# 256 output columns of two row tiles computed behind the input gradient, and the first row tiles flipped in the middle of products

## The chip, the cores and the metric

One core of one Trainium2 chip runs the whole program. The metric is the device time of one execution in microseconds (us); lower is better. Kernels are compared only within the same rounds. A profiled execution has a span of its own, some 2 us shorter than the time measured from outside; spans are compared with spans and times with times.

In the profile PE is TensorE's matmul, PEld its weight load, DVE is VectorE, ACT ScalarE, POOL GpSimd, SP the queue from which most transfers are issued.

## The reference, cut to what matters

The program computes one layer and all its gradients. `S = 2048`, `D = 1024`, `F = 3584`; everything is bfloat16.

```python
xn  = layernorm(x)
y   = A(xn, k, v, ...)              # shift, long convolution, gating by xn
h   = relu(xn @ W_gate) * (xn @ W_up)
out = x + y_branch + h @ W_down      # output 0
# and, from grad_out: the gradients of x (output 1), k, v, the filters and the three weights
```

Three parts matter here. The first block of the hidden stage needs `xn` turned by 128x128 blocks ("flipped"), row tile by row tile, as the layer norm delivers it. `out` needs `h @ W_down`, and nothing else needs `out`. The gradient of `x` is the last stage, and ends for each row tile with the backward pass of the layer norm.

## The kernel before: the parts that matter

A row tile is 128 rows; there are 16. `pin` and `keep_in_program_order` hold an instruction behind the one traced before it on its engine; all others are placed by priority.

The layer norm is a generator in three steps per chunk; the first four chunks are one row tile each, the later ones two.

```python
def layer_norm(self, ...):
    for i, n in enumerate(self.LN_CHUNKS):          # (1, 1, 1, 1, 2, 2, ...)
        for j in range(n):
            total = row_sums(j, 0, ACT.Copy)         # ACT: sum of the row
            if i != 3 and i >= 2 and j == 0:
                self.tc.keep_in_program_order(total)
        ...                                          # mean
        for j in range(n):
            V.tensor_scalar(... op0=ALU.subtract)    # VectorE: x - mean
            row_sums(j, 2, ACT.Square)               # ACT: sum of squares
        yield
        ...                                          # variance, ACT.Sqrt
        yield
        ...                                          # 1/std, VectorE: scale the rows, store xn
        self.xn.append(xt[:, j, :])
        yield
```

A flip is eight transposes on TensorE into PSUM and a copy out of it on VectorE. The first block begins with 24 warm-up products on zeros, then:

```python
def flip(k):                     # flips row tiles until k are there
    while len(xT) < k:
        while len(self.xn) <= len(xT): next(ln)
        xT.append(self.flip_xn(len(xT)))

def first_gate_up(sp):           # two row tiles: gate, up, gate, up; 8 products of 512 columns each
    flip(sp + 1)
    gate(sp)
    flip(sp + 2)                 # before the up product
    while len(self.xn) < 4: next(ln)
    if sp == 2: chunk()          # all three steps of the norm of the fifth and sixth tiles
    up(sp)
    gate(sp + 1)
    up(sp + 1, (lambda: flip(3)) if sp == 0 else None)   # this one sits in the middle of the 8

for _ in range(5): next(ln)
flip(1)
next(ln); next(ln)
first_gate_up(0); first_gate_up(2)
chunk()                          # the norm of the seventh and eighth tiles
# then grad(sp): flip(min(sp + 6, HS)) ahead of the second product group
```

The last two stages: the output takes 2 x 28 products of 512 columns for each row tile, the input gradient 4 x 28; the last tile's second half is cut in two quarters.

```python
def out_phase(...):
    for st in range(16):
        hT = self.tall(h_d, st, "hT")        # transposed load of a row tile of h
        ...
        for ob in range(2):
            for kt in range(28):
                nc.tensor.matmul(ps[:], lhsT=hT[:, kt, :], rhs=self.wd[:, kt, oc], ...)
            nc.vector.tensor_tensor(out=o0[:, oc], in0=ps[:], in1=ya[:, oc], op=ALU.add)

def grad_x(...):
    for st in range(16):
        ggT = self.tall(...); guT = self.tall(...)   # same three buffers as hT
        cuts = (0, 512, 768, D) if last else (0, 512, D)
        ...                                          # products
        ...                                          # backward of the norm: VectorE, ACT, VectorE, store
```

Of the kernel before, what the change touches and what calls it, by code (L numbers as in the profile page):

```python
# [11 lines left out]
BF16 = mybir.dt.bfloat16  # L12
F32 = mybir.dt.float32
I32 = mybir.dt.int32
ALU = mybir.AluOpType
ACT = mybir.ActivationFunctionType
AX = mybir.AxisListType
P = 128
# [640 lines left out]
class LnMlp:  # L659
# [66 lines left out]
    def layer_norm(self, xn_d, jpool, jtag, spool):  # L726
# [4 lines left out]
        for i, n in enumerate(self.LN_CHUNKS):  # L731
# [27 lines left out]
            for j in range(n):  # L759
                total = row_sums(j, 0, ACT.Copy)  # L760
                if i != 3 and i >= 2 and j == 0:
                    self.tc.keep_in_program_order(total)
# [20 lines left out]
            for j in range(n):  # L783
                st = st0 + j
# [68 lines left out]
    def hidden(self, first, goT, load, ln, tables, Wg, Wu, Wd, g, xn_d, h_d, ug_d):  # L853
# [6 lines left out]
        for n in range(N):  # L860
# [61 lines left out]
            def first_gate_up(sp):  # L922

                flip(sp + 1)
                gate(sp)
                yield from step()
                flip(sp + 2)
                while len(self.xn) < 4:
                    next(ln)
                if sp == 2:  # L930
                    chunk()
                up(sp)
                yield from step()
                gate(sp + 1)
                yield from step()
                up(sp + 1, (lambda: flip(3)) if sp == 0 else None)
                yield from step()
# [24 lines left out]
            def grad(sp):  # L962
                for s in (sp, sp + 1):
                    if ahead and s == sp + 1:
                        flip(min(sp + 6, HS))
                    ps = self.ps_tile("ps_h")
                    self.gemm8(ps, gT[s], wd)
                    gh = self.e1_tile("gh")
                    self.pri.pin(nc.scalar.copy(out=gh[:], in_=ps[:]))  # L969
                    self.pri.pin(nc.vector.tensor_tensor(out=ru[s][:], in0=ru[s][:], in1=gh[:].rearrange(  # L970
                        "p (o f) -> p o f", o=1).to_broadcast([P, 2, 512]), op=ALU.mult))

                    def store(r=(s0 + s) * P, cols=cols, t=ru[s]):
                        self.pri.pin(nc.sync.dma_start(out=ug_d[r:r + P, :, cols], in_=t[:]))
                    self.defer(store)
                    yield 1730
                    self.tick()
# [9 lines left out]
            def chunk():  # L987
                with self.tc.issue_after(self.ln_act.ins):
                    for _ in range(3):
                        next(ln)  # L990

            if ahead:
# [4 lines left out]
                next(ln)  # L997
                flip(1)
                next(ln)
                next(ln)  # L1000
# [178 lines left out]

    def out_phase(self, x, xn_d, y_d, h_d, Wg, Wu, out0):  # L1180
        nc, tc, D = self.nc, self.tc, self.D
# [5 lines left out]
        for st in range(self.ST):  # L1187
# [15 lines left out]
            for ob in range(2):  # L1203
                oc = slice(ob * 512, ob * 512 + 512)
                ps = self.ps_tile("ps_o")
                for kt in range(self.FT):
                    nc.tensor.matmul(ps[:], lhsT=hT[:, kt, :], rhs=self.wd[:, kt, oc], start=(kt == 0),  # L1207
                                     stop=(kt == self.FT - 1))
                nc.vector.tensor_tensor(out=o0[:, oc], in0=ps[:], in1=ya[:, oc], op=ALU.add)
            nc.scalar.dma_start(out=out0[rows, :], in_=o0[:])  # L1210
# [3 lines left out]
    def grad_x(self, g, xn_d, y_d, ug_d, out1):  # L1214
# [3 lines left out]
        for st in range(self.ST):  # L1218
# [11 lines left out]
            V.tensor_tensor(out=gy[:], in0=gy[:], in1=gt[:], op=ALU.mult)  # L1230
            gx = p_ev.tile([P, D], F32, name="gx")
# [5 lines left out]
            last = st == self.ST - 1  # L1237
            cuts = (0, 512, 768, D) if last else (0, 512, D)
# [22 lines left out]
            for ob in range(2):  # L1261
# [3 lines left out]
                nc.sync.dma_start(out=out1[rows, oc], in_=o1[:, oc])  # L1265
        p_sm.release()
# [8 lines left out]
def kernel(  # L1275
# [79 lines left out]
    b.grad_x(g, xn_d, y_d, ug_d, out_1[0])  # L1355
# [30 lines left out]
```

## Time and profile before

| | before |
|---|---|
| median of the first 3 runs | 1927.05 us (1924.9 to 1928.51) |
| span of the profiled execution | 1922.2 us |
| granted TensorE clock, mean | 1.000 |
| last product ends, by the trace | 1915.56 us, 6.64 before the end |

The prediction below shows the page's head, the start and the end of the timeline. To those I add the page's list of what TensorE waits for (engine, what it was to do, line, releaser: us in total, times, the longest), cut:

```profile
PE pst_x L837 <- DVE ln_x L787: 2.0, 3, 1.4
PE ps_g L805 <- DMA wg<-in_B_W_gate_dram: 1.3, 3, 0.7
PE ps_g L805 <- DVE xnT L839: 0.4, 1, 0.4
```

The first line is the flips that wait for the norm's scaling (L787), the second the products of the third block that wait for a weight transfer at about 103 us, the third the first gate product that waits for the copy of its flipped tile. They are the waits at which the change aims, and one (the second) at which it doesn't.

One more line, from TensorE's timeline (start, duration, group), is the yardstick for the start of the kernel: the first gate products that use the fifth tile. All of the first block's flips that matter lie before it.

```profile
32.32 3.63 PE L805 MATMUL ps_g<-wg,xnT 128*128 128x512 bf16 x16
```

### The profile page before, as it was taken

Reading aid. Unit: us, or ns where it says so; the run is one execution under the profiler, and the core shown is the slowest. Engines: PE = TensorE matmul, PEld = TensorE weight load, DVE = VectorE, ACT = ScalarE, POOL = GpSimd, SP = SyncE. Lnnn points to the kernel's source line nnn. Section 1 sums busy time; section 2 is a strip of 40 time slices with the busy share of each in tenths; the row PEclk is TensorE's granted clock in tenths of the full one; section 3 lists DMA queues with packets and bytes.
Section 4 is the critical chain, followed back from the end, with each engine's and each line's share of the span. In section 5 each row is a group of like instructions: output and inputs, shape, how many; then the busy total and the mean of one; then the engine's idle time right before and its main releaser. Section 6 shows DMA issues by size and latency. Waiting matters only on the chain.

```text
span 1922.2 us, 36073 instructions
## 1 busy us (share of the span) xinstructions
PE 1888.9 (98%) x15350; PEld 886.8 (46%) x15582; DVE 909.1 (47%) x1366; ACT 635.0 (33%) x867; POOL 15.8 (1%) x38
## 2 busy tenths in 40 slices
PE   9999999999999999999999999999999999999998
PEld 4444444444444444444444444444444444444444
DVE  6777767767767754443444444310222222222222
ACT  5854354364364354354345344321000000000000
POOL 1100000000000000000000000000000000000000
PEclk9999999999999999999999999999999999999999
DMA  9975878974874972655662733386999854554551
GB/s 249 275 180 144 178 184 183 222 188 131 187 186 138 251 215 80 174 132 184 151 165 90 170 99 122 101 208 213 264 248 235 206 128 120 118 120 120 120 119 41
DMA packets 616018, 319.10 MB, mean 166 GB/s; under 512 B 450984, under 2 KB 585136, under 8 KB 615856
## 3 DMA queue, kind: packets, MB, share of 16 engines
q1 hardware_dynamic: 605360, 295.79, 63.6%
q10 hardware_dynamic: 9216, 16.78, 2.9%
q0 software_dynamic: 1280, 4.20, 0.6%
q8 instruction: 122, 2.00, 0.4%
q14 instruction: 40, 0.33, 0.1%
HBM read 141.56 MB, written 95.44 MB: 123 GB/s over the span
## 4 chain that ended last, share of the span: by engine, by line
PE 92%; issue 3%; ACT 2%; DVE 2%; DMA 1%; SPq 1%; ACTq 0%; DVEq 0%
PE ps_w L1053 19%; PE ps_x L1245 19%; PE ps_o L1207 10%; PE ps_h L805 9%; PE ps_u L805 9%; PE ps_g L805 9%; PE ps_d L1053 9%; PE ps L72 7%; PE ps_d L1066 1%; ACT ln_j L743 1%; PE pst L308 0%; PE ps_w L1066 0%; SPq L816 0%; DMA wu<-in_B_W_up_dram 0%; DMA ugs<-ug_d 0%
## 5 line engine op out<-in xcount | busy, mean ns | idle before, releaser
L1053 PE MATMUL ps_w<-ugs,xn_nat 128*128 128x512 bf16 x1672 | 375.9, 379 | 5.8 <-issue 4.3
L805 PEld LDWEIGHTS <-xnT 128*128 128x128 bf16 x1792 | 170.3, 98 | 210.6 <-issue 10.5
L1053 PEld LDWEIGHTS <-xn_nat 128*128 128x128 bf16 x1728 | 165.0, 98 | 199.4 <-issue 5.5
L1263 ACT ACTIVATE w<-xn,m 128x512 f32<-128x512 bf16 x32 | 24.3, 806 | 558.6 <-issue 316.8
L805 PE MATMUL ps_g<-wg,xnT 128*128 128x512 bf16 x869 | 203.8, 379 | 4.4 <-issue 1.6
L805 PE MATMUL ps_u<-wu,xnT 128*128 128x512 bf16 x866 | 203.7, 379 | 3.0 <-issue 1.3
L805 PE MATMUL ps_h<-wdT,goT 128*128 128x512 bf16 x863 | 202.4, 379 | 2.9 <-issue 1.8
L1245 PE MATMUL ps_x<-wgT,ggT 128*128 128x512 bf16 (+1 forms) x907 | 197.8, 372 | 0.9
L1245 PE MATMUL ps_x<-wuT,guT 128*128 128x512 bf16 (+1 forms) x906 | 197.6, 372 | 0.9
L1207 PE MATMUL ps_o<-wd,hT 128*128 128x512 bf16 x878 | 192.6, 379 | 0.9
L1053 PE MATMUL ps_d<-g_nat,hs 128*128 128x512 bf16 x741 | 167.4, 379 | 3.2 <-issue 2.7
L1245 PEld LDWEIGHTS <-ggT 128*128 128x128 bf16 x924 | 90.4, 98 | 103.3
L1245 PEld LDWEIGHTS <-guT 128*128 128x128 bf16 x924 | 90.4, 98 | 103.1
L1207 PEld LDWEIGHTS <-hT 128*128 128x128 bf16 x896 | 87.7, 98 | 105.7
L805 PEld LDWEIGHTS <-goT 128*128 128x128 bf16 x896 | 85.2, 98 | 102.6 <-issue 2.9
L319 DVE STREAM_TRANSPOSE flp<-C 128x1024 f32<-128x1024 f32 x48 | 90.5, 1931 | 83.4 <-ACT C L76 83.4
L908 DVE SCALAR_TENSOR_TENSOR ru<-ru,ps_u 128x512 bf16<-128x512 bf16 x112 | 76.5, 683 | 108.4 <-issue 43.0
L969 ACT CAST gh<-ps_h 128x512 bf16<-128x512 f32 x112 | 65.2, 583 | 164.1 <-PE ps_h L805 147.4
L1157 ACT CAST wi<-ps_w 128x512 bf16<-128x512 f32 x108 | 63.6, 589 | 161.8 <-PE ps_w L1053 153.1
L76 ACT CAST C<-ps 128x1024 bf16<-128x1024 f32 x96 | 92.5, 1015 | 69.0 <-PE ps L72 67.9
L319 DVE STREAM_TRANSPOSE flp<-B 128x1024 f32<-128x1024 f32 x48 | 90.9, 1939 | 48.6 <-ACT B L76 48.6
L1053 PEld LDWEIGHTS <-hs 128*128 128x128 bf16 x768 | 72.7, 98 | 88.9 <-issue 4.2
(170 smaller groups left out, 1469.4 us busy)
## 6 DMA issues: line engine op xcount, KB each, us to landing
ug_d<-ru SPq DMA_DIRECT2D x112, 256.0 KB, 4.0
ugs<-ug_d SPq DMA_DIRECT2D x112, 256.0 KB, 4.4
wg<-in_B_W_gate_dram SPq DMA_DIRECT2D x56, 256.0 KB, 4.4
wu<-in_B_W_up_dram SPq DMA_DIRECT2D x56, 256.0 KB, 4.8
h_d<-ht SPq DMA_DIRECT2D x112, 128.0 KB, 3.5
hs<-h_d SPq DMA_DIRECT2D x56, 256.0 KB, 5.1
out_dram<-wi SPq DMA_DIRECT2D x56, 256.0 KB, 2.5
gt<-in_grad_out_dram SPq DMA_DIRECT2D x32, 256.0 KB, 4.8
```

Source lines behind the costliest of these rows:

```text
L72: self.pri.pin(self.nc.tensor.matmul(out, lhsT=lhsT, rhs=rhs, start=start, stop=stop))
L76: self.pri.pin(self.nc.scalar.copy(out=out, in_=in_))
L319: self.pri.pin(self.nc.vector.transpose(out=df[:, c0:c0 + 32, :], in_=sf[:, c0:c0 + 32, :]))
L743: self.ln_act = nc.scalar.activation(out=jk[:, 0:cut], in_=xt[:, j, 0:cut], func=func, accum_out=sm[:, k, j:j + 1])
L805: self.pri.pin(self.nc.tensor.matmul(ps[:], lhsT=xT[:, kt * P:(kt + 1) * P], rhs=w(kt), start=(kt == 0), stop=(kt == self.DT - 1)), always ...
L908: self.pri.pin(nc.vector.scalar_tensor_tensor(out=ru[s][:, 1, :], in0=ru[s][:, 0, :], scalar=0.0, in1=ps[:], op0=ALU.is_gt, op1=ALU.mult))
L969: self.pri.pin(nc.scalar.copy(out=gh[:], in_=ps[:]))
L1053: self.pri.pin(self.nc.tensor.matmul(ps[:], lhsT=lhsT(st), rhs=rhs(st), start=(st == 0), stop=(st == self.ST - 1)))
L1157: self.pri.pin(nc.scalar.copy(out=wo[0][:, d, :], in_=ps[:]))
L1207: nc.tensor.matmul(ps[:], lhsT=hT[:, kt, :], rhs=self.wd[:, kt, oc], start=(kt == 0), stop=(kt == self.FT - 1))
L1245: nc.tensor.matmul(ps, lhsT=T[:, kt, :], rhs=W[:, kt, oc], start=(i == 0), stop=(i == n - 1))
L1263: nc.scalar.activation(out=w[:, oc], in_=xn[:, oc], func=ACT.Identity, scale=m[:, 7:8], bias=m[:, 6:7])
```

## The change

Two independent intents:

- **End.** The last 256 columns of the last two row tiles of the output are left out of the output stage and computed after the last input-gradient product, so that TensorE has work while the last backward pass of the norm runs on ACT and VectorE. Their weights, which the output stage's buffer no longer holds by then, are loaded again (1.8 MB) in the second input-gradient tile. The last tile is no longer cut in quarters.
- **Start.** The flips of the first tiles go from between two product groups into the middle of one (`gemm8` calls `mid` after four of eight products), so that each tile has 0.86 us more to arrive; the steps of the norm are traced in another order, and the second tile's row sum is pinned behind the first tile's square root.

The diff, cut to its core:

```diff
 # layer_norm
-                if i != 3 and i >= 2 and j == 0:
+                if i != 3 and i >= 1 and j == 0:
                     self.tc.keep_in_program_order(total)
 # first_gate_up
                 flip(sp + 1)
+                if sp == 2:
+                    chunk(1)
                 gate(sp)
                 yield from step()
-                flip(sp + 2)
-                while len(self.xn) < 4:
+                if sp == 0:
                     next(ln)
-                if sp == 2:
-                    chunk()
-                up(sp)
+                    next(ln)
+                    next(ln)
+
+                def mid():
+                    flip(sp + 2)
+                    while len(self.xn) < 4:
+                        next(ln)
+                    if sp == 2:
+                        chunk(2)
+                up(sp, mid)
 # grad
-                    if ahead and s == sp + 1:
-                        flip(min(sp + 6, HS))
                     ps = self.ps_tile("ps_h")
-                    self.gemm8(ps, gT[s], wd)
+                    self.gemm8(ps, gT[s], wd, (lambda: flip(min(sp + 6, HS))) if ahead and s == sp + 1 else None)
 # start of the first block
                 next(ln)
-                next(ln)
                 flip(1)
-                next(ln)
-                next(ln)
                 yield from first_gate_up(0)
 # out_phase
-            for ob in range(2):
-                oc = slice(ob * 512, ob * 512 + 512)
+            end = D if st < self.ST - 2 else D - self.REST          # REST = 256
+            for c0 in range(0, end, 512):
+                oc = slice(c0, min(c0 + 512, end))
 # new
+    def rest_load(self, x, xn_d, y_d, Wd):                          # called in tile 1 of grad_x
+        self.wdr = self.p_rest.tile([P, self.FT, self.REST], BF16, name="wdr")
+        for a in range(0, self.FT, 7):
+            nc.sync.dma_start(out=self.wdr[:, a:a + 7, :], in_=Wd[...])
+        t = self.p_rest.tile([P, 3, 2, self.REST], BF16, name="rest")
+        for i, src in enumerate((y_d, xn_d, x)):
+            nc.sync.dma_start(out=t[:, i], in_=src[(self.ST - 2) * P:self.S, c0:D]...)
+        ...                                                         # y * xn + x
+    def rest_out(self, h_d, out0):                                  # called after the last tile of grad_x
+        for i in range(2):
+            st = self.ST - 2 + i
+            hT = self.tall(h_d, st, "hT")
+            for kt in range(self.FT):
+                ins = nc.tensor.matmul(ps, lhsT=hT[:, kt, :], rhs=self.wdr[:, kt, :], ...)
+            nc.vector.tensor_tensor(out=t[:, 1, i], in0=ps, in1=t[:, 0, i], op=ALU.add)
+            nc.sync.dma_start(out=out0[st * P:(st + 1) * P, c0:D], in_=t[:, 1, i])
 # grad_x
-            cuts = (0, 512, 768, D) if last else (0, 512, D)
+            cuts = (0, 512, D)
```

More of the change, by code (lines that the diff above doesn't have):

```diff
@@ L985, in grad, with chunk @@
                         late.pop(0)()
-            def chunk():
+            def chunk(steps=3):
                 with self.tc.issue_after(self.ln_act.ins):
-                    for _ in range(3):
+                    for _ in range(steps):
                         next(ln)
@@ L1178, in tall @@
         return t
+    REST = 256
     def out_phase(self, x, xn_d, y_d, h_d, Wg, Wu, out0):
@@ L1202, in out_phase @@
             o0 = p_ev.tile([P, D], BF16, name="o0")
-            for ob in range(2):
-                oc = slice(ob * 512, ob * 512 + 512)
-                ps = self.ps_tile("ps_o")
+            end = D if st < self.ST - 2 else D - self.REST
+            for c0 in range(0, end, 512):
+                oc = slice(c0, min(c0 + 512, end))
+                ps = self.ps_tile("ps_o")[:, 0:oc.stop - c0]
                 for kt in range(self.FT):
-                    nc.tensor.matmul(ps[:], lhsT=hT[:, kt, :], rhs=self.wd[:, kt, oc], start=(kt == 0),
+                    nc.tensor.matmul(ps, lhsT=hT[:, kt, :], rhs=self.wd[:, kt, oc], start=(kt == 0),
@@ L1208, in out_phase @@
                                      stop=(kt == self.FT - 1))
-                nc.vector.tensor_tensor(out=o0[:, oc], in0=ps[:], in1=ya[:, oc], op=ALU.add)
-            nc.scalar.dma_start(out=out0[rows, :], in_=o0[:])
+                nc.vector.tensor_tensor(out=o0[:, oc], in0=ps, in1=ya[:, oc], op=ALU.add)
+            nc.scalar.dma_start(out=out0[rows, 0:end], in_=o0[:, 0:end])
         p_ev.release()
         self.p_wd.release()
-    def grad_x(self, g, xn_d, y_d, ug_d, out1):
+    def rest_load(self, x, xn_d, y_d, Wd):
+        nc, D, c0 = self.nc, self.D, self.D - self.REST
+        self.p_rest = self.tc.alloc_tile_pool(name="x_rest", bufs=1, side="right")
+        self.wdr = self.p_rest.tile([P, self.FT, self.REST], BF16, name="wdr")
+        for a in range(0, self.FT, 7):
+            nc.sync.dma_start(out=self.wdr[:, a:a + 7, :],
+                              in_=Wd[a * P:(a + 7) * P, c0:D].rearrange("(kt p) o -> p kt o", p=P))
+        t = self.p_rest.tile([P, 3, 2, self.REST], BF16, name="rest")
+        for i, src in enumerate((y_d, xn_d, x)):
+            nc.sync.dma_start(out=t[:, i], in_=src[(self.ST - 2) * P:self.S, c0:D].rearrange("(t p) o -> p t o", p=P))
+        nc.vector.tensor_tensor(out=t[:, 0], in0=t[:, 0], in1=t[:, 1], op=ALU.mult)
+        nc.vector.tensor_tensor(out=t[:, 0], in0=t[:, 0], in1=t[:, 2], op=ALU.add)
+        self.rest = t
@@ new lines, in rest_out @@
+    def rest_out(self, h_d, out0):
+        nc, D, c0, t = self.nc, self.D, self.D - self.REST, self.rest
+        for i in range(2):
+            self.pri.now()
+            st = self.ST - 2 + i
+            hT = self.tall(h_d, st, "hT")
+            ps = self.ps_tile("ps_r")[:, 0:self.REST]
+            for kt in range(self.FT):
+                ins = nc.tensor.matmul(ps, lhsT=hT[:, kt, :], rhs=self.wdr[:, kt, :], start=(kt == 0),
+                                       stop=(kt == self.FT - 1))
+                if kt == 0:
+                    self.tc.keep_in_program_order(ins)
+            nc.vector.tensor_tensor(out=t[:, 1, i], in0=ps, in1=t[:, 0, i], op=ALU.add)
+            nc.sync.dma_start(out=out0[st * P:(st + 1) * P, c0:D], in_=t[:, 1, i])
@@ L1215, in grad_x @@
+    def grad_x(self, x, g, xn_d, y_d, h_d, ug_d, Wd, out0, out1):
         nc, tc, D, V = self.nc, self.tc, self.D, self.nc.vector
@@ L1230, in grad_x @@
             V.tensor_tensor(out=gy[:], in0=gy[:], in1=gt[:], op=ALU.mult)
+            if st == 1:
+                self.rest_load(x, xn_d, y_d, Wd)
             gx = p_ev.tile([P, D], F32, name="gx")
@@ L1236, in grad_x @@
             hd = tc.keep_in_program_order
-            last = st == self.ST - 1
-            cuts = (0, 512, 768, D) if last else (0, 512, D)
+            cuts = (0, 512, D)
             for ob in range(len(cuts) - 1):
@@ L1265, in grad_x @@
                 nc.sync.dma_start(out=out1[rows, oc], in_=o1[:, oc])
+        self.rest_out(h_d, out0)
+        self.p_rest.release()
         p_sm.release()
@@ L1354 @@
     b.out_phase(x, xn_d, y_d, h_d, B_W_gate, B_W_up, out_0[0])
-    b.grad_x(g, xn_d, y_d, ug_d, out_1[0])
+    b.grad_x(x, g, xn_d, y_d, h_d, ug_d, B_W_down, out_0[0], out_1[0])
 _INS = ['A_q', 'A_k', 'A_v', 'A_shift_k', 'A_ssm_k', 'A_ssm_D', 'B_x', 'B_W_gate', 'B_W_up', 'B_W_down', 'grad_out']
```

## The prediction

The sum comes to -3.3 us for the end and -1.9 for the start, -5.2 together, from 1927.05 about 1922. The 216 and 109 ns per product and the 2.71 us of the last store in it are read from the trace of before.

> **What bounds the kernel now.** I read the page first, then the waits of TensorE, then its timeline over the first 60 us, then the timeline of all engines over the last 60 us, then the DMA issues. From the page:
>
> ```profile
> span 1922.2 us, 36073 instructions
> PE 1888.9 (98%) x15350; PEld 886.8 (46%) x15582; DVE 909.1 (47%) x1366; ACT 635.0 (33%) x867; POOL 15.8 (1%) x38
> PEclk9999999999999999999999999999999999999999
> ```
>
> TensorE is busy for 98% of the span at an ungated clock, so only two things can move the end: the number and width of its products, and the places where it stands still. The page says how little is there to win: 1922.2 - 1888.9 = 33 us of TensorE not busy in all, and part of those are records missing from the trace. The change touches two places, the start and the end. The start, in TensorE's own timeline (start, duration, group, and in brackets the idle time before it):
>
> ```profile
> 8.92 0.61 PE L837 MATMUL pst_x<-ident,ln_x 128*128 128x128 bf16 x8
> 9.96 1.90 PE L805 MATMUL ps_g<-wg,xnT 128*128 128x512 bf16 x8 [0.43 <-DVE xnT L839]
> 11.92 0.62 PE L837 MATMUL pst_x<-ident,ln_x 128*128 128x128 bf16 x8
> 15.83 1.03 PE L805 MATMUL ps_u<-wu,xnT 128*128 128x512 bf16 x4
> 17.01 0.62 PE L837 MATMUL pst_x<-ident,ln_x 128*128 128x128 bf16 x8 [0.15 <-DVE ln_x L787]
> 17.46 1.03 PE L805 MATMUL ps_u<-wu,xnT 128*128 128x512 bf16 x4
> 18.41 1.90 PE L805 MATMUL ps_g<-wg,xnT 128*128 128x512 bf16 x8
> 20.72 0.62 PE L837 MATMUL pst_x<-ident,ln_x 128*128 128x128 bf16 x8 [0.40 <-DVE ln_x L787]
> 26.36 1.89 PE L805 MATMUL ps_h<-wdT,goT 128*128 128x512 bf16 x8
> 29.65 1.07 PE L837 MATMUL pst_x<-ident,ln_x 128*128 128x128 bf16 x16 [1.41 <-DVE ln_x L787]
> 30.56 1.89 PE L805 MATMUL ps_h<-wdT,goT 128*128 128x512 bf16 x7
> ```
>
> The durations hold a modelled tail, so I count starts. Eight 512-wide products take 1.73 us from start to start (as from 14.10 to 15.83), eight transposes 0.45. By that count TensorE loses 0.59 us after the first tile's flip (8.92 + 0.45 to 9.96), 0.23 before the second tile's (9.96 + 1.73 to 11.92), 0.32 before the third's, 0.09 before the products at 18.41, 0.58 before the fourth's and 1.56 before the fifth's and sixth's. All of them wait for the layer norm, a chain over ACT and VectorE; between 9.96 and 30.56 that is 2.78 us. The end, from the timeline of all engines:
>
> ```profile
> 1902.96 3.15 PEld L1245 LDWEIGHTS <-ggT 128*128 128x128 bf16 x28
> 1912.34 3.22 PE L1245 MATMUL ps_x<-wuT,guT 128*128 128x256 bf16 x28
> 1915.60 0.42 DVE L1247 CUSTOM_DVE_ANT_0 gx<-ps_x,gy 128x256 f32<-128x256 f32 x1 [4.62 <-PE ps_x L1245]
> 1917.25 1.52 ACT L1263 ACTIVATE w<-xn,m 128x512 f32<-128x512 bf16 x2 [22.27 <-issue]
> 1918.09 1.40 DVE L1264 TENSOR_TENSOR o<-gx,w 128x512 bf16<-128x512 f32 x2 [0.55 <-ACT w L1263]
> ```
>
> The last product ends at 1915.56; then the layer norm's backward chain runs alone to 1918.09 + 1.40 = 1919.49, and a store to 1922.2: 6.64 us in which TensorE has nothing to do, 3.93 of chain and 2.71 of store.
>
> [...] 28 weight loads at full width span 6.04 us (216 each) and the half-width groups of the last tile 3.05 (109). Halving the width thus costs almost nothing in rate. [...] the first tile's copy out of PSUM starts at 9.49, only after two small layer-norm operations of the second tile (9.23 and 9.42) that stood ahead of it. [...]
>
> **The change, part by part.**
> Moved products. The last two row tiles of the output lose 256 of 1024 columns: per tile 28 products of 216 ns become 28 of 109, 6.04 to about 3.1 us, -5.8 us for two. They come back at the very end as 2 x 28 of 109 ns = 6.1 us, with some 0.1 for each change of group (the first half-width group took 3.15, later ones 3.05): 6.2. The last input-gradient tile is no longer cut in 512+256+256: its four half-width groups (3.15 + 3.05 x 3 = 12.3) become two full ones (12.1), -0.2. Sum on TensorE +0.2, close to nothing.
> The tail. The backward chain of the last tile (4.4 us at full width, by the tile before: 1891.29 to 1894.31 + 1.40) now lies beside 6.2 us of products. After the last product there remain one 256-wide addition from PSUM (0.42 us, as its neighbour of that width at 1915.60) and the store (2.7). So 3.93 becomes about 0.46: -3.5 us. Together with the +0.2: -3.3.
> The start. The first copy need no longer stand behind the second tile's variance: about -0.14 (copy at 9.35 in place of 9.49; the flip itself cannot come before 8.92, since the warm-up's last product starts at 8.71). Each flip then comes four products (0.86 us) later among the products, which covers the 0.23 wholly, and part of the 0.32 and 0.58: I take -0.23, -0.1, -0.4. The fifth and sixth tiles' sums are put ahead of a gate product, from 20.85 to about 18.8 on ACT, and their flips 0.86 later: 2.9 us of slack against a 1.56 us wait, of which I take -1.3, since ACT and VectorE, both some 70% busy there, may lose some of it. Against it: a flip in the middle leaves only 0.86 us until its tile is used, and the flip's own end plus a 0.69 us copy need 0.95 (17.46 to 18.41 now): +0.09 for two more tiles, and 0.1 where the copy finds VectorE busy. Sum -1.9.
> Sum of all: -3.3 - 1.9 = -5.2 us, from 1927.05 about 1922.
>
> **Rivals.** (1) A transposed load takes the place of the tail. The last rest product needs the last tile of h, whose buffer comes free when the last tile has used its gate gradient for the second time, 18.1 us into the tile; the product comes at 24.2 + 3.1 = 27.3. From the DMA issues:
>
> ```profile
> hT<-h_d SPq DMA_TRANSPOSE x16, 9.7
> guT<-ug_d SPq DMA_TRANSPOSE x16, 6.8
> ```
>
> 9.2 us are there against 6.8 for such a load in this stage (9.7 where other transposes ran beside it). I hold it for covered; if not, 0.5 to 2 us of the gain go: 1923 to 1924. [...]
> (2) The extra loads disturb the input gradient: 1.8 MB of weights plus 0.4 MB are queued during its second tile, ahead of that tile's transposed load. At some 200 GB/s, which the DMA row of the page shows elsewhere, 11 us, in a stage that moves only 115-120 GB/s; the load behind it has 12 us from issue to use. A stall of 1 to 2 us is possible, once. [...]
> (3) The start gains nothing: the norm chain is a chain, and if TensorE arrives earlier it waits for the next tile, or at the next weight block, whose weights already keep it waiting three times for 1.3 us in sum between 100 and 107 us while the DMA share is at its full. Then only the tail counts: 1924.
> (4) The start gains all 2.8 us, and the tail as said: 1921.
>
> **Range and chances.** The three times before lie between 1924.9 and 1928.5, so a median of few runs is uncertain by 1 to 2 us, as large as most of the terms. The centre is 1922.0; 8 in 10: 1918.5 to 1926. Two per cent are 38.5 us: more than all the time TensorE is not busy, so faster by over 2% can be all but ruled out; slower by over 2% would need the new order to upset the instruction stream of the middle 1800 us, which the change leaves alone and whose products are pinned in order.
>
> **What would show it.** Right: the last products are half-width and end 3 to 3.5 us before the span does, with a single addition and a store after them; the last tile's ACT pair lies beside products; TensorE busy stays within 1 us of 1888.9 but for missing records; the product group that now starts at 32.32 starts between 29.8 and 31. Wrong: idle time before the rest products with the transposed load of h as its releaser; an idle entry of some us in the second or third tile of the input gradient; longer waits for copies (xnT) before gate products in the first 30 us; or the waits for weights around 103 us grown by what the start gained.

## The result, and the profile after

Ratios are the mean time of one kernel's runs over the mean of the other's in the same rounds, so they are not quite the ratios of the medians quoted beside them.

| | before | after |
|---|---|---|
| first comparison, median | 1926.31 us (4 runs) | 1922.07 us (1919.92 to 1925.05, 4 runs) |
| ratio, 95% interval | | 0.9978 (0.9959 to 0.9997) |
| second comparison (run after_again), median | 1925.19 us (9 runs) | 1920.76 us (1919.8 to 1922.78, 5 runs) |
| ratio, 95% interval | | 0.9978 (0.9965 to 0.9992) |
| span of the profile | 1922.2 us | 1918.5 us |

So the change takes off 0.22%, some 4.2 us of 1926, in both comparisons. By the 2% measure that is "same"; the intervals show that it is real. The prediction was 1922.0, a gain of 5.2 us from 1927.05.

The head of the page of after:

```profile
span 1918.5 us, 36320 instructions
PE 1909.4 (100%) x15582; PEld 886.9 (46%) x15582; DVE 910.2 (47%) x1364; ACT 635.8 (33%) x867; POOL 15.7 (1%) x38
```

TensorE's busy time seems to have grown by 20 us. It hasn't: the trace of before holds 15350 of 15582 matmul records, this one all of them. The weight loads are complete in both, 886.8 and 886.9 us, and say that the work on TensorE is the same.

**The end**, from the timeline of all engines:

```profile
1908.62 6.21 PEld L1244 LDWEIGHTS <-hT 128*128 128x128 bf16 x56
1908.84 6.28 PE L1244 MATMUL ps_r<-wdr,hT 128*128 128x256 bf16 x56
1911.22 1.52 ACT L1301 ACTIVATE w<-xn,m 128x512 f32<-128x512 bf16 x2 [22.65 <-issue]
1913.01 0.68 DVE L1302 TENSOR_TENSOR o<-gx,w 128x512 bf16<-128x512 f32 x1
1915.15 0.42 DVE L1248 TENSOR_TENSOR rest<-ps_r,rest 128x256 bf16<-128x256 f32 x1 [1.46 <-PE ps_r L1244]
```

The 56 half-width products end at 1908.84 + 6.28 = 1915.12; the ACT pair and the last VectorE addition of the norm's backward pass lie beside them and are done at 1913.69. What is left is one 256-wide addition and a store. From the last product to the end it is now 1918.5 - 1915.12 = 3.38 us, before it was 6.64. There is no bracket on the product line: they waited for nothing.

**The start**, from TensorE's timeline (in brackets the idle time before the group and what ended it):

```profile
9.63 0.61 PE L837 MATMUL pst_x<-ident,ln_x 128*128 128x128 bf16 x8
...
17.59 0.62 PE L837 MATMUL pst_x<-ident,ln_x 128*128 128x128 bf16 x8 [0.30 <-DVE ln_x L787]
...
21.60 0.61 PE L837 MATMUL pst_x<-ident,ln_x 128*128 128x128 bf16 x8
22.05 1.03 PE L805 MATMUL ps_u<-wu,xnT 128*128 128x512 bf16 x4
23.79 1.90 PE L805 MATMUL ps_g<-wg,xnT 128*128 128x512 bf16 x8 [0.71 <-DVE xnT L839]
...
29.84 1.06 PE L837 MATMUL pst_x<-ident,ln_x 128*128 128x128 bf16 x16
...
31.62 3.63 PE L805 MATMUL ps_g<-wg,xnT 128*128 128x512 bf16 x16
```

The waits for the norm are gone before the second flip, before the fourth (21.60) and before the fifth and sixth (29.84, 1.56 us by starts before). The third still waits, and a new wait stands before the fourth tile's gate product: its four up products start at 22.05 and take 0.86 us, so it could start at 22.91 and starts at 23.79. The list of waits says the same in sums, and shows the wait for the weights grown from 1.3 to 1.6 us:

```profile
PE ps_g L805 <- DMA wg<-in_B_W_gate_dram: 1.6, 1, 1.6
PE ps_g L805 <- DVE xnT L839: 1.0, 2, 0.7
PE pst_x L837 <- DVE ln_x L787: 0.3, 1, 0.3
```

Waits for the norm and the copies went from 2.4 to 1.3 us, and the fifth tile's gate product starts at 31.62 in place of 32.32.

**Where the span's 3.7 us went.** Last product 1915.56 to 1915.12: 0.44 us from the start, less the grown weight wait and some 0.2 us of extra products. Behind the last product: 3.26 us. The gain is nearly all the end's.

### The profile page after: what moved, and what is told of

It reads as the page before. It is cut to its first block, busy times and chain, and to the rows that moved or that the text cites. A ratio compares the mean times of both kernels' runs of the same rounds, so it can differ in the third digit from the quotient of the medians.

```text
span 1918.5 us, 36320 instructions
## 1 busy us (share of the span) xinstructions
PE 1909.4 (100%) x15582; PEld 886.9 (46%) x15582; DVE 910.2 (47%) x1364; ACT 635.8 (33%) x867; POOL 15.7 (1%) x38
## 4 chain that ended last, share of the span: by engine, by line
PE 96%; DVE 1%; ACT 1%; DMA 1%; issue 0%; POOL 0%; SPq 0%; ACTq 0%; POOLq 0%
PE ps_x L1283 20%; PE ps_w L1056 20%; PE ps_o L1214 10%; PE ps_h L805 9%; PE ps_u L805 9%; PE ps_g L805 9%; PE ps_d L1056 9%; PE ps L72 7%; PE ps_d L1069 1%; PE ps_w L1069 1%; ACT ln_j L743 1%; PE ps_warm L851 0%; PE pst L308 0%; PE ps_r L1244 0%; DMA wg<-in_B_W_gate_dram 0%
## 5 line engine op out<-in xcount | busy, mean ns | idle before, releaser
L1056 PE MATMUL ps_w<-ugs,xn_nat 128*128 128x512 bf16 x1728 | 383.9, 379 | 0.0
L1283 PE MATMUL ps_x<-wgT,ggT 128*128 128x512 bf16 x896 | 198.6, 379 | 0.0
L1283 PE MATMUL ps_x<-wuT,guT 128*128 128x512 bf16 x896 | 198.6, 379 | 0.0
L1214 PE MATMUL ps_o<-wd,hT 128*128 128x512 bf16 (+1 forms) x896 | 187.6, 372 | 0.0
L1056 PE MATMUL ps_d<-g_nat,hs 128*128 128x512 bf16 x768 | 172.1, 379 | 0.0
```

The source lines that it names most:

```text
L1056: self.pri.pin(self.nc.tensor.matmul(ps[:], lhsT=lhsT(st), rhs=rhs(st), start=(st == 0), stop=(st == self.ST - 1)))
L1214: nc.tensor.matmul(ps, lhsT=hT[:, kt, :], rhs=self.wd[:, kt, oc], start=(kt == 0), stop=(kt == self.FT - 1))
L1283: nc.tensor.matmul(ps, lhsT=T[:, kt, :], rhs=W[:, kt, oc], start=(i == 0), stop=(i == n - 1))
```

## The experiments

The theory after the result: the end gives what was predicted; the start gives less than half, because a copy now stands behind other VectorE work and one flip still waits. Rivals: the start did gain, but the weight wait at 103 us takes it back; or the start is bound by something not yet seen. Twelve runs. Each variant shares its rounds with the kernel before.

### 1. The change again, and its parts alone

`after_again` is the changed kernel. `tail_only` keeps the new end and has the old start; `start_only` the reverse (the edits are the two halves of the diff above, undone). `one_rest` leaves 256 columns of one tile instead of two for the end:

```diff
-            end = D if st < self.ST - 2 else D - self.REST
+            end = D if st < self.ST - 1 else D - self.REST
-        t = self.p_rest.tile([P, 3, 2, self.REST], BF16, name="rest")
+        t = self.p_rest.tile([P, 3, 1, self.REST], BF16, name="rest")
         ...                                                         # rows of one tile loaded, not of two
-        for i in range(2):
-            st = self.ST - 2 + i
+        for i in range(1):
+            st = self.ST - 1 + i
```

> The changed kernel once more, to tell its gain from the spread of single executions (four runs lay between 1919.9 and 1925.1 us). Theory (tail -3.3 us, start -0.7 to -1.4, nothing given back): 4 to 4.7 us below the kernel before. Rival (the start's gain is given back at the weights waited for near 103 us, only the tail counts): about 3.3. Profile: 3.4 us from the end of the last product to the end of the span; from the first flip to the first gate product of the fifth tile 22.0 us (23.4 before), whatever the moment at which the warm-up ends.

> The start as before, the output's last columns moved behind the input gradient. Theory: -3.3 us against the kernel before, all of it in the tail (6.6 us from last product to end become 3.4), first flip to the fifth tile's gate product 23.4 us as before. Rival (the tail was not what was gained, the moved products cost as much as they hide): within 1 us of before.

> The flips in the middle of products and the new order of the norm, the end as before. Theory: -0.7 to -1.4 us against the kernel before; first flip to the fifth tile's gate product 22.0 us; 6.6 us from last product to end. Rival (later waits for weights take it back): 0, with the waits for wg near 103 us grown by about 1 us over the 1.3 us of before.

> Only the last row tile leaves 256 columns, so 28 half-width products (3.1 us) follow the last input-gradient tile in place of 56 (6.2 us). Theory: the last tile's backward chain (4.4 us) is then longer than the products beside it; the additions of the input gradient are the last work again, the end comes about 4.4 + 0.4 + 2.7 us after the last input-gradient product, and the time is 0.7 to 1.1 us above the changed kernel. Rival (any products behind the last tile do, since the store sets the end): the same time as the changed kernel.

| run | median us (range, 5 runs) | ratio to before (95%) | span |
|---|---|---|---|
| after_again | 1920.76 (1919.8 to 1922.78) | 0.9978 (0.9965 to 0.9992) | 1919.0 |
| tail_only | 1921.41 (1920.34 to 1922.8) | 0.9981 (0.9969 to 0.9994) | 1919.5 |
| start_only | 1924.42 (1923.96 to 1926.38) | 0.9997 (0.9985 to 1.001) | 1924.6 |
| one_rest | 1921.49 (1919.48 to 1925.13) | 0.9982 (0.9969 to 0.9994) | 1917.7 |

The end alone is worth 0.19%, 3.7 us of 1925.19; the start alone 0.03%, 0.6 us, which its interval doesn't tell from nothing. The two add up to the whole within the noise. One expectation failed: from the first flip to the fifth tile's gate product I foresaw 22.0 us whatever the moment at which the warm-up ends; it took 22.54 in `after_again` and 22.65 in `start_only` (the account of the prediction below says why).

`one_rest` shows why two tiles and not one. From its timeline:

```profile
1909.88 3.15 PEld L1244 LDWEIGHTS <-hT 128*128 128x128 bf16 x28
1914.26 0.68 DVE L1302 TENSOR_TENSOR o<-gx,w 128x512 bf16<-128x512 f32 x1
```

The 28 products are over by about 1913.3, but the backward pass ends at 1914.94: it is longer than what lies beside it, and sets the end again. To put sizes on one scale I take, for each variant, the time from the first of the moved products to the end, less what the output stage saved. What was saved is read from the length of the output stage, 193.4 us before. For after: 9.88 - 5.9 = 4.0. For `one_rest`: 7.82 - 2.9 = 4.9, so 0.9 worse. (Its profile has the shortest span of all for other reasons: its wait for the weights at 103 us was only 1.19 us. Its time over five runs is not better.)

### 2. The copy behind other work, and the weights at 103 us

In after, VectorE does this around the fourth tile's copy:

```profile
22.25 0.88 DVE L766 TENSOR_SCALAR ln_x<-ln_x,ln_s 128x1024 bf16<-128x1024 bf16 x2 [0.33 <-DVE ln_s L764]
23.05 0.68 DVE L839 COPY xnT<-pst_x 128x1024 bf16<-128x1024 bf16 x1
```

The transposes start at 21.60. Before, the copy followed the same transposes after 0.66 us (20.72 and 21.38), which would be 22.26 here. But the subtraction for the fifth and sixth tiles (two instructions) stands ahead of it, because the change traces `chunk(1)` before that flip and the copy is kept in program order. On ACT, the third tile's square root is late in the same way, behind the fourth tile's row sum:

```profile
14.53 1.04 ACT L743 ACTIVATE ln_j<-ln_x 128x1024 bf16<-128x1024 bf16 x1
15.57 0.19 ACT L774 ACTIVATE ln_s<-ln_b 128x1 f32<-128x1 bf16 x1
```

`split4_pin3` mends both: the row sum is pinned behind the root, and the subtraction is traced after the copy.

```diff
-                if i != 3 and i >= 1 and j == 0:
+                if i >= 1 and j == 0:
                     self.tc.keep_in_program_order(total)
             ...
+            if i == 4:
+                yield
             for j in range(n):
-                V.tensor_scalar(out=xt[:, j, :], ..., op0=ALU.subtract)
+                centred = V.tensor_scalar(out=xt[:, j, :], ..., op0=ALU.subtract)
+                if i == 4 and j == 0:
+                    self.tc.keep_in_program_order(centred)
             ...
-                        chunk(2)
+                        chunk(3)
```

`wgfirst_after` and `wgfirst_before` test the rival on the changed and the old kernel. On the SP queue, the transfer of the third block's gate weights stands behind a load of `xn` for the other branch, which is issued late. The edit moves that load and the load after it behind the weights, without touching the order of the arithmetic:

```diff
-        yield 13000
+        yield 21990
         self.load_xn(nx)
         ...
-        yield 9000
+        yield 10
```

`all3` is `split4_pin3` and this edit together.

> The changed kernel with the two waits of its start taken away by order alone: the subtraction of the fifth and sixth tiles' means stands behind the fourth tile's copy out of PSUM on VectorE (it stood ahead of it, and the gate product after it waited 0.71 to 0.72 us), and the fourth tile's row sum stands behind the third tile's square root on ACT (it stood ahead of it, and the third flip waited 0.30 to 0.77 us). Theory: first flip to the fifth tile's gate product 21.99 - 0.8 - 0.4 = 20.8 us, the time 1 us below the changed kernel's. Rival (the norm is one chain, so what is taken from one tile's wait comes back at the next): 21.7 us or more, the time unchanged.

> The changed kernel; on the queue of transfers the load of normalised rows that waits for their store (4.4 us near 90) and what follows it stand behind the weights of the third block in place of ahead of them; the compute engines' order is the same. Theory: TensorE's wait for these weights near 103 us (1.2 to 2.4 us in six profiles, in one of them followed by a stretch at a lower clock) goes, and with it part of the spread: 1 to 2.5 us below the changed kernel, 5.5 to 7 below the kernel before. Rival (the wait comes from the transfer engines' load at that time, not from the place in the queue): wait and time as in the changed kernel.

> The same move in the kernel before, to see whether the change's gain depends on this wait. Theory (the wait moves along with TensorE and takes nothing back of the change's gain): 1 to 2.5 us below the kernel before, and the kernel of the same move with the change stays 4 to 4.8 us below this one. Rival (the wait takes back the gain of the start): the difference between the two with the move is 1 us larger than without it, 5 to 6 us.

> Both mends of the changed kernel together (the two orders of the start, the weights of the third block first). Theory: they add up: 7 us below the kernel before, near 1918. Rival: no better than the better of the two alone.

| run | median us (range, 5 runs) | ratio to before (95%) | span |
|---|---|---|---|
| split4_pin3 | 1922.68 (1920.83 to 1924.27) | 0.9978 (0.9965 to 0.9992) | 1922.4 |
| wgfirst_after | 1921.73 (1921.19 to 1923.75) | 0.9978 (0.9966 to 0.9991) | 1922.0 |
| wgfirst_before | 1924.44 (1924.26 to 1926.67) | 0.9993 (0.998 to 1.0005) | 1922.6 |
| all3 | 1921.55 (1921.03 to 1922.51) | 0.9976 (0.9963 to 0.9988) | 1919.2 |

Before in these rounds: 1926.3, 9 runs.

`split4_pin3` did half of what it was to do. In it the fourth tile's gate product starts at 22.75, 1.04 us earlier than in after (and earlier than in any of the seven profiles with the change's start, 23.31 to 23.79), but it still waits 0.63 us: only the first of the two subtractions was pinned behind the copy, and the scheduler put the other one ahead. The fifth tile's gate product starts at 31.05 with a wait of 0.33 for its copy. From the first flip to the fifth tile's gate product it is 22.99 us, where I had expected 20.8, and the time didn't move: the rival held. My theory of the copies explains the waits, not the time: the mended wait came back in part as a later one.

For the weights, `wgfirst_after` did remove the wait for `wg`. TensorE's list of waits between 86 and 115 us now begins with another:

```profile
PE ps_u L805 <- DMA wu<-in_B_W_up_dram: 2.0, 2, 1.8
```

The gate weights were issued at 94.65 in place of 98.89, but the `up` weights only at 102.50, behind the loads that had been moved. In this profile, then, the wait passed from one weight to the next. Between 100 and 110 us, without the move, the sixteen transfer engines are at their full share, 1.08 to 1.12 by the profile's windows, and move 294 to 329 GB/s (start_only, after and tail_only); that this load sets the wait is not shown. For in `wgfirst_before` the wait for `wu` is only 0.7 us, and in `all3` the list from 90 to 130 us has no weights at all (one group of its up products does take 2.48 us from start to start in place of 1.73), and still the time moved by nothing that is clear of the noise. In these two TensorE waits for VectorE's transposes of the other branch instead (`flp`, 2.0 and 1.8 us from 115 us on), a wait that before and after don't have: what was gained was waited for again later. The forecasts for `all3` (1918) and `wgfirst_after` (1 to 2.5 us below the changed kernel) failed; their rivals held. The two kernels with the move differ by 2.7 us (medians), which neither my 4 to 4.8 nor the rival's 5 to 6 had: taking this wait away uncovers no hidden gain of the start.

Does this wait give back what the start gained? The load of `xn` that stands first was issued 0.61 us after the other branch's transposes began on TensorE, before (94.78 and 95.39) and after (94.25 and 94.86), and 0.61 to 1.23 in the other profiles with the queue's old order; the gate weights followed it at 99.52 before and 98.89 after, 0.63 earlier. So their issue moves along with TensorE, by as much as the start gained. The rival doesn't hold as a systematic effect, though the wait itself varies between profiles from 1.0 to 2.4 us: when the transfer lands, the traces don't explain.

### 3. All copies first; flips alone; other widths

`copies_first` goes further with the copies: both subtractions of chunks 4 and 5 are pinned behind the copies, and the norm of the seventh and eighth tiles is traced later.

```diff
-            if i == 4:
+            if i in (4, 5):
                 yield
             ...
-                if i == 4 and j == 0:
+                if i in (4, 5):
                     self.tc.keep_in_program_order(centred)
             ...
                 yield from first_gate_up(2)
-                chunk()
+                chunk(1)
             ...
                 yield from grad(sp)
+                if ahead and sp == 0:
+                    chunk(3)
```

(against `split4_pin3`). `flip_mid` moves only the flips into the middle of products, with the steps of the norm that are traced beside them, and leaves the norm's order and pins as in the kernel before; it has the new end. `rest128` and `rest512` leave 128 and 512 columns for the end (`REST = 128`, `REST = 512`).

> The changed kernel; on VectorE both subtractions of the fifth and sixth tiles' means stand behind the fourth tile's copy out of PSUM, both of the seventh and eighth behind the fifth's and sixth's copies, and the fourth tile's row sum on ACT behind the third tile's square root (in the first try at this only one of two subtractions was moved, and a gate product still waited 0.61 to 0.63 us for its copy). Theory: the waits for copies (0.71 to 0.72 us before the fourth tile's gate product, 0 to 0.87 before the fifth's) go, the fifth tile's gate product starts near 30.5 to 30.8 us in place of 31.2 to 32.3, the time is about 1 us below the changed kernel's. Rival (the norm is one chain; what is put off for the copies makes later flips wait): the product at 31.2 or later, or the seventh tile's flip waits; time as the changed kernel.

> Only one part of the start: the flips go into the middle of products, the order of the norm stays as before; the end is the changed kernel's. Compare with the kernel that has the old start and the new end (fifth tile's gate product at 32.54 us, waits for normalised rows of 2.7 us). Theory: a flip that comes 0.86 us later waits that much less, but the chain before it is as late as before: the waits for rows fall to about 1 us and the copies now cost 0.1 to 0.7 each; the fifth tile's gate product near 31.9, 0.5 to 0.7 us of the start's gain. Rival A (the middle flips are the whole gain): near 31.6 or below, as in the changed kernel. Rival B (the norm's new order is the whole gain): 32.4.

> Only 128 columns of the last two tiles at the end, so 56 products 128 wide follow. Theory: at 57 ns each, as the flips run, they take 3.2 us, less than the 4.4 us of the backward chain beside them, which becomes the end again: 0.8 to 1.3 us above the changed kernel. Rival (the weight load of 98 ns sets the pace of so narrow products): they take 5.5 us and end after the chain, but the tiles of the output gain only 3 us for it: 2.4 us above the changed kernel.

> 512 columns of the last two tiles at the end: 56 full-width products, 12.1 us, behind the last input-gradient tile, and 3.7 MB of weights and 0.8 MB of rows loaded during its second tile in place of 2.2 MB. Theory: the tail is one addition of 512 columns (0.69 in place of 0.42 us) and a store of twice the size, 0.3 to 0.5 us more; if the loads run at the 200 GB/s or so of the changed kernel (2.2 MB from 1530.5 to 1542.3) they take 22 us and the second tile's transposed load, queued behind them, is late: a wait of 2 to 6 us appears before a product of the second or third tile, in sum 2 to 6 us above the changed kernel. Rival (the loads do not get in the way of the transposed one): 0.3 to 0.5 us above.

| run | median us (range, 5 runs) | ratio to before (95%) | span |
|---|---|---|---|
| copies_first | 1921.14 (1920.17 to 1922.26) | 0.9975 (0.9962 to 0.9988) | 1920.5 |
| flip_mid | 1923.3 (1921.12 to 1925.82) | 0.9984 (0.997 to 0.9997) | 1921.8 |
| rest128 | 1922.62 (1920.7 to 1926.73) | 0.9985 (0.9972 to 0.9997) | 1921.6 |
| rest512 | 1921.83 (1921.53 to 1922.77) | 0.9979 (0.9966 to 0.9991) | 1919.7 |

Before in these rounds: 1926.31, 9 runs.

**`copies_first`** removes every listed wait between the first copy and the fifth and sixth flips, and then stops. TensorE, and ACT's row sum for the seventh tile:

```profile
22.34 1.90 PE L809 MATMUL ps_g<-wg,xnT 128*128 128x512 bf16 x8
28.39 1.06 PE L841 MATMUL pst_x<-ident,ln_x 128*128 128x128 bf16 x16
32.37 3.63 PE L809 MATMUL ps_g<-wg,xnT 128*128 128x512 bf16 x16 [2.05 <-DVE xnT L843]
```

```profile
28.32 1.06 ACT L743 ACTIVATE ln_j<-ln_x 128x1024 bf16<-128x1024 bf16 x1 [2.72 <-DMA ln_x<-in_A_q_dram]
```

TensorE is 1.45 us earlier than in after, both at the fourth tile's gate product (22.34 for 23.79) and at the fifth and sixth flips (28.39 for 29.84), and the fifth tile's gate product is none the earlier: 32.37, where the kernel before had 32.32. ACT had run out of rows: it could go on with those of the seventh and eighth tiles only at 28.3 us. On VectorE, the step of their norm that follows stood ahead of the copies for the fifth and sixth tiles again. Here the start runs into a load. It is visible in other profiles too. Wherever else ACT had to wait for those rows, the fifth tile's gate product came a fixed time after ACT went on:

| run | ACT goes on | fifth tile's gate product | between |
|---|---|---|---|
| after | 26.85 | 31.62 | 4.77 |
| start_only | 26.78 | 31.55 | 4.77 |
| wgfirst_after | 27.57 | 32.34 | 4.77 |
| rest512 | 27.88 | 32.65 | 4.77 |
| all3 | 26.71 | 31.49 | 4.78 |

In after, the chain between is short enough to read: ACT's two row sums, VectorE's mean (29.07) and subtraction (29.48, 0.88 us), then a product of the gradient (30.28), then the two copies (30.88). In the kernel before, ACT was busy until 27.5 us with other work, so a landing at 27 could not be seen. The load isn't the limit everywhere: in after TensorE's own work would have let the product start at 30.74 + 0.86 = 31.60, so it lost nothing, and in after_again, one_rest and rest128 ACT did not wait for the rows at all. TensorE's wait for the copies behind it was 0.23 us in start_only, 0.83 in all3, 0.87 in wgfirst_after, 1.37 in rest512 and 2.05 here. Part of the lateness lies on the SP queue: the load stands there behind transposed loads, whose issuing instructions ended at 20.3 us in after and at 23.1 here; it was issued at 20.46 and 23.23, and ACT went on 6.39 and 5.09 us later (6.08 in start_only, issued at 20.70). No run shows what an earlier issue would bring.

**`flip_mid`** shows that moving flips is not enough. The fifth and sixth flips still wait 1.13 us for the norm and the gate product behind them 0.99 us; it starts at 32.91, later than in the kernel before, and later than my 31.9 and both rivals had it. The gain of the start needs the norm's new order as well.

**The widths.** On the scale of experiment 1 (time from the first moved product to the end, less what was saved): `rest128` 8.1 - 2.9 = 5.2, `one_rest` 4.9, after 4.0, `rest512` 16.2 - 12.0 = 4.2. With 3.1 and 3.3 us of products beside it the backward pass, 4.4 us long, sticks out; with 6.2 it is covered, and more products bring nothing. From the timeline of `rest128`:

```profile
1913.51 3.33 PEld L1244 LDWEIGHTS <-hT 128*128 128x128 bf16 x56
1918.27 0.28 DVE L1248 TENSOR_TENSOR rest<-ps_r,rest 128x128 bf16<-128x128 f32 x1
```

Its 56 products cost 3.3 us, under 60 ns each, although each weight load by itself is recorded with 98 ns: loads overlap, and I had held it possible that they don't. The end is late because the last addition (1918.27) stands behind the backward pass on VectorE, not for the products. The width of the last store hardly matters: from the end of the last addition to the end of the span it is 3.05 us with 32 KB (`rest128`), 2.93 with 64 (after) and 3.02 with 128 (`rest512`). In `rest512` the larger reload might have held up the input gradient's transposed load, and 2 to 6 us were expected for that. In the trace the instruction that issues this load takes 9.68 us, in after 3.59, but TensorE waits only 0.23 us for it:

```profile
1547.05 5.82 PEld L1283 LDWEIGHTS <-guT 128*128 128x128 bf16 x28 [0.23 <-DMA guT<-ug_d]
```

So doubling the moved work, and the bytes, costs some 0.2 us on this scale: the choice of 256 columns of two tiles is at the edge of a flat stretch. The times order the same way (0.9978 and 0.9979 against 0.9982 and 0.9985), but no two of these intervals are apart.

None of the twelve beats the changed kernel clearly; `copies_first` (0.9975) and `all3` (0.9976) lie within its interval.

## Why the prediction was right, and the step that was mis-sized

**Right.** The bound: TensorE, busy for 98% and 100% of the span at a mean granted clock of 1.000, in both kernels. The term for the end, -3.3 us: it was to be -3.5 behind the last product and +0.2 on TensorE, and is -3.26 and +0.2 by the traces (6.21 us of products at the end, 5.87 saved in the output stage, 0.12 in the last tile); in time, by `tail_only`, -3.7. The signs named for it are all there: half-width products last, one addition and a store behind them, the ACT pair beside them. The time, 1922.0 predicted and 1922.07 and 1920.76 measured, is closer than the working deserves, and that is luck: the gain was to be 5.2 us and was 4.2, but the kernel before came out at 1926.31 and 1925.19 beside it in place of 1927.05.

**Rival 1** (the transposed load of `h` takes the tail's place) is refuted: it was issued at 1902.99, its bytes had moved by 1908.2, 5.2 us later where I had allowed 6.8, and no product waited. **Rival 2** (the extra loads disturb the input gradient) is refuted too: no wait in that stage in after, and with twice the bytes, in `rest512`, 0.23 us.

**The mis-sized term is the start, -1.9 us; it measured about -0.7.** The fifth tile's gate product was to start between 29.8 and 31. Over the three profiles with the old start (before, tail_only, wgfirst_before) it starts at 32.41 on average, over the seven with the new start as it is in the change (after, after_again, start_only, one_rest, wgfirst_after, rest128, rest512) at 31.69, from 31.16 to 32.65. Measured in time, `start_only` says -0.6. Term by term, in the trace of after:

| step, as predicted | predicted | in after |
|---|---|---|
| first copy ahead of the second tile's variance | -0.14 | -0.14 |
| second flip's wait | -0.23 | -0.23 |
| third flip's wait | -0.1 | +0.14 (0.32 to 0.46 by starts) |
| fourth flip's wait | -0.4 | -0.58 |
| fifth and sixth flips' wait | -1.3 | -1.56 |
| two copies too late by 0.09 | +0.18 | +0.09 (second tile) |
| a copy that finds VectorE busy | +0.1 | +0.87 (fourth tile, its own 0.09 included) |

The sum is -1.4 in that trace (-1.9 predicted), and that is also what the distance from the first flip to the fifth tile's gate product lost (23.40 to 21.99). In that execution the warm-up ended 0.71 us later than in before (first flip at 9.63 for 8.92), which leaves -0.7. But a late warm-up isn't why the average is -0.7 too. The third flip is held by the norm and not by the warm-up: it starts at 17.11 to 17.59 us in the seven profiles with the new start and at 17.01 to 17.23 in the three with the old one, and when the first flip comes earlier it only waits longer (0.30 us in after, 0.77 in after_again). So whatever was gained ahead of it is lost there: that is the first step that failed, "part of the 0.32" for the third flip. From the third flip to the fifth tile's gate product the change takes 14.0 us in place of 15.3, or more where the load of the seventh and eighth tiles is late (14.4 to 15.5 in three of the seven).

The second step that failed is "0.1 where the copy finds VectorE busy". I had seen the mechanism, and named longer waits for copies as a sign of being wrong, but had not read from the diff what VectorE would be busy with: the change itself traces the fifth and sixth tiles' subtraction ahead of that copy. And the third flip was not helped, since the change pins the row sums of other chunks but not the fourth tile's; with that sum pinned too it starts at 16.53 to 16.87 (`all3`, `split4_pin3`, `copies_first`).

`split4_pin3` and `copies_first` show that this isn't the whole cause either. With those waits wholly or partly gone, the time stays where it was. In `copies_first` the traces show why for the start: the rows of the seventh and eighth tiles let ACT go on only at 28.3 us, and their norm stands ahead of the copies that TensorE needs. In `split4_pin3` ACT did not wait for them; there the product starts at 31.05, 0.6 us ahead of the seven's average, and why the time shows nothing of it stays open. No rival had this. **Rival 3** (the start gains nothing, 1924): by time it isn't refuted, since `start_only`'s 0.6 us can't be told from nothing; by the traces the start gains 0.7 us by the fifth tile, and its reason, the weights at 103 us, is not the cause: their issue moves along with TensorE. **Rival 4** (all of 2.8 us) is refuted by the traces.

**Open.** The spread of 1 to 6 us between executions is as large as the effects. Three parts of it are seen in the traces: the warm-up, the landing of the rows, and, at 103 us, a clock that sometimes halves. The 24 warm-up products, the same in all variants, took from 6.67 to 8.31 us, and the first flip moved with them from 8.06 to 9.63 us (but in `tail_only`, where it waited for the norm); the third flip hides most of that here. In `start_only` TensorE stood still for 2.29 us up to 103.80, and then, by windows of 1 us (stretch and its length; busy time and count of PE, PEld, DVE, ACT, POOL; clock, transfer share, GB/s), of which one is:

```profile
106.00:107.00 1.00, 1.00 (x4) 0.39 (x3) 1.00 (x2) 0.00 (x0) 0.00 (x0) 0.50 1.10 364
```

From 105 to 108.4 us the clock was half: the mean over 100 to 110 us is 0.83, in after 1.00, and 0.17 of 10 us is 1.7 us. Four of the fourteen profiles (`start_only`, `flip_mid`, `copies_first`, `rest128`) have a mean of 0.83 there, and `wgfirst_after` 0.96 with 0.86 in the next ten, so five in all. In all five TensorE had stood still for 1.8 to 2.3 us just before (in `copies_first` in two parts, 0.84 and 1.16), and the clock was down for the equivalent of 3.4 to 3.6 us at half; but `tail_only` and `split4_pin3` stood still there for 2.16 and 2.02 us and kept a clock of 1.00. What makes the clock fall is not shown. Part of why `copies_first` shows a longer span than after is probably this, and not its order. How often it strikes each kernel in unprofiled runs can't be told from a handful, so I don't correct the times for it.

## What to carry to other kernels

When TensorE is the bound, the end of a program is where the other engines' last chain lies bare (here 3.93 us of chain, then 2.71 of store): put independent products behind the last dependent ones, as many as the trailing chain on the other engines is long, here about 4.4 us: 3.1 and 3.3 us of products left it bare, 6.2 covered it, and 12.1 brought nothing more. When an instruction is moved later to give its producer time, ask what else the program order then puts ahead of its consumer: a copy of 0.7 us behind 0.9 us of someone else's subtraction ate 0.8 us of this gain. An earlier start of the consumer was worth nothing, either, where the producer set the moment, as at the third flip (17.11 to 17.59 us with the new start, 17.01 to 17.23 with the old). And when waits are taken out one by one and the time doesn't follow, look upstream for a load whose late landing the old waits may have hidden (here ACT could go on only at 26.7 to 28.3 us).
